# An eighteenth seven-product group, partial outputs kept in PSUM, and a port lock in the scheduler of a convolution-and-joint kernel

## The chip, the cores and the metric

The kernel runs on one core of one Trainium2 chip. Its time is the device time in microseconds (us). Before the change it is 260.56 us, the median of 3 runs (260.44 to 260.65).

## The reference

Two strided convolutions with gelu, then a "joint": every frame is added to every one of 8 label states, goes through tanh and one 512x512 product.

```python
B, T, D, K, U = 2, 4000, 512, 5, 8
h = gelu(conv5(x, w1))[:, ::2]            # 2000 frames
f = gelu(conv5(h, w2))[:, ::2]            # 1000 frames
fe = einsum("btd,de->bte", f, w_f)
ge = einsum("bud,de->bue", g, w_g)
j = tanh(fe[:, :, None, :] + ge[:, None, :, :])
return einsum("btud,dv->btuv", j, w_o)    # 16000 rows of 512
```

## The kernel before

All engines work from one list of operations. The program gives each operation a cost, a list scheduler plans the order on each engine, and semaphores follow from what is read and written. The joint's 16000 rows are 125 tiles of 128. A plain tile takes 4 matmuls of 512 columns. Four neighbouring tiles can also be done as a *group*: a seven-product scheme on 2x2 blocks, with 28 matmuls of 256 columns in place of 16 of 512, paid for by additions on other engines. `WQ` lists the groups done so. Groups below 14 have their operand sums on VectorE, the later ones on GpSimd (POOL). TensorE writes its products into PSUM, which the program uses as eight banks of 512 columns (tile name `acc`); the other engines copy or add them from there into SBUF, the working memory. Later products can add onto what a bank holds. The parts that matter here, cut:

```python
WQ = (5,6,10,11,12,13,16,17,18,20,21,22,23,24,26,27,28)      # 17 groups
LEAD, TRAIL = 4,4            # plain tiles ahead of and behind the late groups
...
def op(self, eng, fn, reads=(), writes=(), cost=0.1):         # one operation in the plan
...
        def quad_steps(q, eng, u=[0]):
            ...
            def sums():      # eight 128x256 (or four 128x512) additions, two SBUF inputs each
                ...
            def one():
                held.extend(banks.pop(0) for _ in range(3))
                x, y, z = held
                product(Ab(0, 0), Bb(0, 0), x, True)      # product: 4 matmuls of 256 columns
                product(Sb(1), Tb(1), y, True)
                act(k1, v2(x), ACT.Copy)
                tt("dve", u2, v2(y), k1, add)             # PSUM + SBUF -> SBUF
            def two():
                product(Sb(0), Tb(0), z, True)
                product(Ab(0, 1), Bb(1, 0), x, False)
                tt("dve", k15, v2(z), k1, add)
                act(half(0, 0), v2(x), ACT.Copy)          # half: a quarter of the output
            def three():
                product(Sb(2), Tb(2), y, False)
                product(Sb(3), Bb(1, 1), z, False)
                tt("dve", half(1, 1), v2(y), k15, add)
                tt("dve", half(0, 1), v2(z), u2, add)
            def four():
                product(Ab(1, 1), Tb(3), y, False)
                tt("dve", half(1, 0), v2(y), k1, add)
            return [sums, one, two, three, four]
...
        def joint_tile(jt):
            ...
                by_act = h == 1 if last else jt % 2 == 0 if end else jt % 3 == 2 if early else plain[0] % 3 == 2
                # the copy out of PSUM: by ScalarE if by_act, else by VectorE; then an output transfer
...
        def weights_o(wT):   # four sums of the joint's weights, on VectorE
```

The convolution units (`stages`) run on the same engines, with joint tiles as filling between their steps. `fe(0)` and `fe(1)` are the products with w_f.

Of the kernel before, what the change touches and what calls it, by code (L numbers as in the profile page):

```python
# [7 lines left out]
ACT = mybir.ActivationFunctionType  # L8
# [4 lines left out]
P = 128  # L13
# [3 lines left out]
class View:  # L17


    __slots__ = ("ap", "cells", "psum")  # L20
# [41 lines left out]


class Op:
    __slots__ = ("eng", "fn", "reads", "writes", "dma", "signal", "count", "sem", "val", "idx", "cost", "pin", "after", "nbytes", "rate")


class Plan:
# [11 lines left out]
    def op(self, eng, fn, reads=(), writes=(), cost=0.1):  # L80
        o = Op()
        o.eng, o.fn, o.dma, o.signal, o.idx = eng, fn, False, False, len(self.ops)
        o.reads, o.writes, o.cost, o.pin, o.after = tuple(reads), tuple(writes), cost, eng in self.pin, []
        self.ops.append(o)
        return o

    def dma(self, eng, fn, reads=(), writes=(), sem=None, nbytes=524288, rate=300e3):

        o = Op()
        o.eng, o.fn, o.dma, o.signal, o.idx = eng, fn, True, False, len(self.ops)  # L90
        o.reads, o.writes, o.after, o.nbytes = tuple(reads), tuple(writes), [], nbytes
        o.cost, o.pin = (1.35, False) if eng == "pool" else (0.05, True)
        o.rate = rate
        if sem is None:
            sem = [self.nc.alloc_semaphore(f"s_d{o.idx}"), 0]
        sem[1] += 16
        o.sem, o.val = sem[0], sem[1]
        self.ops.append(o)
        return o
# [91 lines left out]
    def simulate(self, pred, succ, late):  # L191


        ops, HOP = self.ops, self.HOP
        n = len(ops)
        left = [len(p) for p in pred]
        ready = [0.0] * n
        free = {e: 0.0 for e in ("pe", "act", "dve", "pool", "sp")}
        cand = {e: [] for e in free}
        for i in range(n):  # L200
            if not left[i]:
                cand[ops[i].eng].append(i)
        order = {e: [] for e in free}
        wire, soft, start = 0.0, 0.0, [0.0] * n
        for _ in range(n):
            best = None
            for e, c in cand.items():
                if c:
                    t = max(free[e], min([ready[i] for i in c]))
                    if best is None or t < best[0]:  # L210
                        best = (t, e)
            t, e = best
            now = [i for i in cand[e] if ready[i] <= t + 0.02]
            i = min(now) if e in ("pe", "sp") else min(now, key=lambda i: (late[i], i))
            cand[e].remove(i)
            order[e].append(i)
            o = ops[i]
            start[i] = t
            free[e] = t + o.cost
            end = free[e]  # L220
            if o.dma and e == "pool":
                soft = max(soft, end + 3.0)
                busy = wire > soft + 1.0
                soft += o.nbytes / (60e3 if busy else 230e3)
                wire += o.nbytes / 220e3 if busy else 0.0
                end = max(soft, end + 4.0)
            elif o.dma:
                wire = max(wire, t + 1.3) + o.nbytes / o.rate
                end = max(wire, t + 2.0)
            for s in succ[i]:  # L230
                ready[s] = max(ready[s], end + HOP if pred[s][i] else free[e])
                left[s] -= 1
                if not left[s]:
                    cand[ops[s].eng].append(s)
        return order, start, max(free.values())
# [75 lines left out]
def bass_standalone__seq2seq_rnn_t_joint__speech_kernel(  # L311
# [27 lines left out]
    XW = 528  # L339
    HOFF, HWID = 2, 338  # L340
    RING, LRING = 2048, 4096
    WQ = (5,6,10,11,12,13,16,17,18,20,21,22,23,24,26,27,28)
    LEAD, TRAIL = 4,4
    FROM, LATE = 64 * P, 30
    NSLOT = 12
    BU = B * U
# [4 lines left out]
    with ExitStack() as es:  # L351
# [163 lines left out]
        for pp in range(2):  # L515
            for rt in range(2):
                bk = 4 + 2 * pp + rt
                pv = View(psb[:, bk * 1024:(bk + 1) * 1024].rearrange("p (r k c) -> p r k c", r=2, k=NK), np.array([bk]), True)

                def fn(e, rt=rt, pp=pp, pv=pv):  # L520
                    for r in range(2):
                        for k in range(NK):
                            ins = e.transpose(pv.ap[:, r, k, :], xr[rt].h[:, 2 * r + pp, k, :], ident.h[:, :])
                    return ins
                pl.op("pe", fn, (xr[rt][:], ident[:]), (pv,), 0.8)
                o = xs[0][pp::2, :, 16 + rt * P:16 + (rt + 1) * P]
                if pp:
                    act(o, pv, ACT.Copy)
                else:
                    pl.op("dve", lambda e, o=o, pv=pv: e.tensor_copy(out=o.ap, in_=pv.ap), (pv,), (o,), vec_cost(o, (pv,)))  # L530


        def shift(src, off, dst, c0, n, which):
# [104 lines left out]

        banks = [0, 1, 2, 4]
        fbanks = [3, 5, 7, 6]  # L640
        class Tile_:
            def __init__(self, b, src, dst, c0, i0, n, keep=False):
                self.b, self.i0, self.n, self.keep = b, i0, n, keep
# [12 lines left out]
            def gelu(self, m, src):  # L656
                j = HOFF + self.i0 // 3
                o = hT[self.b][:, m, j:j + self.n // 3].map(
                    lambda a: a.rearrange("p (r s) q -> p s r q", s=2))
                src = src.map(lambda a: a.rearrange("p s (q r) -> p s r q", r=3))  # L660
                act(o, src, ACT.Gelu_apprx_tanh)

            def gelu1(self, m, s, src):
                j = HOFF + self.i0 // 3
# [53 lines left out]
        class Triple:  # L718
# [64 lines left out]
            def stages(self, m, split=None):  # L783
                n, u = self.n, post_n[0]
                post_n[0] += 1
                e, f_at = banks.pop(0), []
                E = ps.cols(e * NT, n)
                F = lambda: ps.cols(f_at[0] * NT, n)
                k1, k2, y = ((sd4[m] if split else sd[u % 2])[i, 0:n] for i in range(3))
# [16 lines left out]

                def two():
                    self.product("t2", m, e, False)
                    f_at.append(banks.pop(0))
                    stt("dve", F(), E, 2.0 * f_, k2)  # L810
                    tt("dve", k1, k1, k2, add)
                    stt("dve", y, E, f_, k1)
                    self.out(1, m, y)
# [157 lines left out]
        pl.pin = ()  # L971


        def bank():
            banks.append(banks.pop(0))
            return banks[-1] * NT

        def ge():
            c0 = bank()
            bank()  # L980
            for m in range(NK):
                mm(ps.cols(c0 + m * BU, BU), [(wg_sb[k, m * P:(m + 1) * P], gT[k]) for k in range(NK)], True, True)
            act(geT[:], ps.cols(c0, NK * BU), ACT.Copy)

        def fe(b):
            for i, m in ((1, 0), (0, 0), (1, 1), (0, 1), (2, 0), (2, 1), (1, 2), (0, 2), (2, 2), (1, 3), (0, 3), (2, 3)):
                v = ps.cols(bank(), START[i + 1] - START[i])
                sl = slice(START[i], START[i + 1])
                mm(v, [(wf_sb[k, m * P:(m + 1) * P], fT[b][k, sl]) for k in range(NK)], True, True)
                o = feT[b][m, i::3]  # L990
                if i == 1:
                    act(o, v, ACT.Copy, cost=0.45)
                else:
                    pl.op("dve", lambda e, o=o, v=v: e.tensor_copy(out=o.ap, in_=v.ap), (v,), (o,), 0.475)  # L994
# [72 lines left out]
        def joint_tile(jt):  # L1067
# [10 lines left out]
            for h in range(2 if last else 1):  # L1078
                w = NT // 2 if last else NT
                cl = slice(h * w, (h + 1) * w)  # L1080
                v = ps.cols(bank(), w)
                mm(v, [(j(k), wo_sb[k, cl]) for k in range(NK)], True, True)
                o = oste[s, cl] if s < 4 else ostq[s - 4, cl] if s < 16 else ostm[s - 16][cl]
                end = jt > ntile - 6
                by_act = h == 1 if last else jt % 2 == 0 if end else jt % 3 == 2 if early else plain[0] % 3 == 2
                if by_act:
                    act(o, v, ACT.Copy)
                else:
                    pl.op("dve", lambda e, o=o, v=v: e.tensor_copy(out=o.ap, in_=v.ap), (v,), (o,), vec_cost(o, (v,)))  # L1089
                send(c0, s, cl, "act" if end and by_act else "sp")  # L1090

        def weights_o(wT):
# [3 lines left out]
            tt("dve", T_[1], B_[1][1], T_[0], sub)  # L1096
            tt("dve", T_[2], B_[1][1], B_[0][1], sub)
            tt("dve", T_[3], B_[1][0], T_[1], sub)

        def quad_steps(q, eng, u=[0]):  # L1100

# [72 lines left out]
            def four():  # L1174
# [4 lines left out]
                banks.append(y)  # L1179
                send2(c0 + 2 * P, s1, s0 + 2)  # L1180

            return [sums, one, two, three, four]

        fes = [1]
        one_tile = lambda jt: (lambda: joint_tile(jt), 1)
        for q in range(14):
            if q in WQ:
                st = quad_steps(q, "dve")
                work.insert(len(work) - (1 if q < 8 else 3), (st[0], 0))
                if q == 13:  # L1190
                    work.append((lambda: weights_o(wT), 0))
                work.extend((f, 1) for f in st[1:])
            else:
                work.extend(one_tile(jt) for jt in range(4 * q, 4 * q + 4))
        left = [jt for jt in range(56, ntile) if jt // 4 not in WQ]
        lateq = [quad_steps(q, "pool") for q in WQ if q >= 14]
        n = len(lateq)
        stream = []
        for i in range(n + 1):
# [114 lines left out]
```

## Time and profile before

In the profile lines PE is TensorE's matmuls, PEld its weight loads (the stationary operands), DVE VectorE, ACT ScalarE, POOL GpSimd. A timeline line gives start and length in us, engine, source line, operation, tiles (written <- read), shape and count, and in brackets how long the engine stood idle before it and what released it; `...` marks lines left out. Tiles: `sA`, `sAm` are operand sums of groups, `wT`, `wTm` sums of the joint's weights, `kq`, `kqm` partial outputs kept in SBUF, `oste`, `ostq`, `ostm` outputs on their way out, `jT`, `jL` the joint's tanh values, `hT` and `fT` the convolutions' outputs, `sd`, `row` and `r` values between the convolutions' steps.

Stages are cut at starts of matmuls in the trace: *head* is from the span's start to the first fe(0) matmul, *middle* from there to the first fe(1) matmul (conv2 and the groups up to 13), *fe(1)* its own matmuls, *tail* from the last fe(1) matmul to the end of the last matmul, *end* from there to the end of the span.

| stage, us | before | before, run again |
|---|---|---|
| head | 79.11 | 78.85 |
| middle | 112.31 | 112.32 |
| fe(1) | 6.68 | 6.67 |
| tail | 57.71 | 57.85 |
| end | 2.83 | 2.83 |
| span | 258.64 | 258.52 |

### The profile page before, as it was taken

How to read it: one execution, taken by the hardware profiler on the slowest of the kernel's cores; microseconds unless marked ns; L12 is line 12 of the kernel's file. 1: busy time of each engine (PE TensorE's matmuls, PEld its weight loads, DVE VectorE, ACT ScalarE, POOL GpSimd, SP SyncE). 2: the span in 40 equal slices, each digit the busy share in tenths (PEclk: the TensorE clock that was granted, in tenths of full speed). 3: DMA queues.
4: the chain of work that ended last, by engine and by line, in shares of the span. 5: the costliest groups of instructions: out<-in, count | busy, mean ns of one | idle time of the engine just before them, and what ended most of it. 6: DMA issues, size and time to landing. Idle time of an engine off the chain costs nothing.

```text
span 258.6 us, 4891 instructions
## 1 busy us (share of the span) xinstructions
PE 252.5 (98%) x1772; PEld 171.4 (66%) x1786; DVE 227.1 (88%) x446; ACT 189.7 (73%) x317; POOL 56.0 (22%) x64
## 2 busy tenths in 40 slices
PE   8998999999999999999999999999999999999995
PEld 4897764446666556565677754777776677777772
DVE  1999999999999999999647899999957698898974
ACT  2778979975366999667765659848549999999631
POOL 1000004300000000000000000000001999999940
DMA  6999998979995022102111031404120264545457
GB/s 239 329 161 190 255 311 181 166 138 187 235 188 103 3 81 81 63 20 71 54 41 66 19 122 42 145 0 144 41 81 4 80 205 143 185 138 179 152 166 242
DMA packets 56277, 33.95 MB, mean 131 GB/s; under 512 B 31150, under 2 KB 55998, under 8 KB 56254
## 3 DMA queue, kind: packets, MB, share of 16 engines
q1 hardware_dynamic: 53710, 31.22, 45.2%
q0 software_dynamic: 2112, 2.10, 4.7%
q8 instruction: 14, 0.23, 0.4%
q10 hardware_dynamic: 432, 0.33, 0.4%
q14 instruction: 9, 0.07, 0.1%
HBM read 7.86 MB, written 16.38 MB: 94 GB/s over the span
## 4 chain that ended last, share of the span: by engine, by line
PE 88%; DMA 5%; SPq 3%; DVE 1%; issue 1%; ACT 0%; DVEq 0%
PE acc L430 88%; SPq L461 3%; DMA w_sb<-in_w_dram 2%; DMA xs<-in_x_dram 1%; DMA xr<-in_x_dram 1%; DMA out_dram<-ostq 1%; DVE kq L417 0%; DVE ty L598 0%; DVE xt L417 0%; DVE ostq L417 0%; DVE w_t L598 0%; ACT fT L422 0%; ACT cs L422 0%; ACT oste L422 0%; SPq L448 0%
## 5 line engine op out<-in xcount | busy, mean ns | idle before, releaser
L430 PE MATMUL acc<-wo_sb,jT 128*128 128x512 bf16 (+1 forms) x199 | 45.0, 353 | 0.5
L1147 POOL TENSOR_TENSOR sA<-jL 128x512 f16<-128x512 bf16 x22 | 25.1, 1158 | 87.5 <-ACT jL L422 85.4
L422 ACT ACTIVATE jT<-feT,geT 128x1000 bf16<-128x1000 f32 (+9 forms) x56 | 40.6, 779 | 3.2 <-PE acc L430 2.1
L422 ACT ACTIVATE jL<-feT,geT 128x1000 bf16<-128x1000 f32 (+3 forms) x36 | 35.8, 1054 | 0.6 <-DVE feT L994 0.6
L417 DVE TENSOR_TENSOR ostq<-acc,kq 128x512 bf16<-128x512 f32 x45 | 29.6, 682 | 3.2 <-PE acc L430 3.0
L430 PEld LDWEIGHTS acc<-wo_sb,jT 128*128 128x128 bf16 x208 | 20.2, 98 | 15.6 <-ACT jT L422 0.2
L430 PE MATMUL acc<-wo_sb,jL 128*128 128x256 bf16 (+1 forms) x155 | 28.9, 313 | 0.3
L430 PE MATMUL acc<-xt,w_sb 128*128 128x252 bf16 (+1 forms) x144 | 23.5, 305 | 0.0
L417 DVE TENSOR_TENSOR kq<-acc,kq 128x512 f32<-128x512 f32 x30 | 19.6, 683 | 3.9 <-PE acc L430 2.6
L422 ACT ACTIVATE hT<-acc 128x334 bf16<-128x334 f32 (+3 forms) x33 | 15.1, 465 | 10.1 <-PE acc L430 10.0
L1089 DVE CAST oste<-acc 128x512 bf16<-128x512 f32 (+1 forms) x25 | 16.9, 684 | 4.6 <-PE acc L430 4.5
L430 PE MATMUL acc<-row,w_sb 128*128 128x334 bf16 (+1 forms) x112 | 20.5, 305 | 0.0
L430 PEld LDWEIGHTS acc<-wo_sb,jL 128*128 128x128 bf16 x160 | 15.5, 98 | 7.1
L430 PE MATMUL acc<-wT,sA 128*128 128x256 f16 x144 | 20.1, 273 | 0.0
L422 ACT ACTIVATE sd<-acc 128x334 f32<-128x334 f32 (+1 forms) x32 | 13.9, 446 | 7.2 <-PE acc L430 6.9
L430 PEld LDWEIGHTS acc<-xt,w_sb 128*128 128x128 bf16 x144 | 14.0, 98 | 7.0 <-DVE xt L417 0.3
L430 PE MATMUL acc<-zx,w_sb 128*128 128x334 bf16 (+1 forms) x96 | 17.6, 305 | 0.0
L422 ACT ACTIVATE ostq<-acc 128x512 bf16<-128x512 f32 x20 | 12.5, 623 | 6.2 <-PE acc L430 3.8
L430 PEld LDWEIGHTS acc<-wT,sA 128*128 128x128 f16 x144 | 14.1, 98 | 3.8
L430 PE MATMUL acc<-xs,w_t 128*128 128x252 bf16 (+1 forms) x76 | 14.0, 314 | 0.7 <-ACT cs L422 0.7
L430 PE MATMUL acc<-row,w_t 128*128 128x334 bf16 (+1 forms) x80 | 14.6, 305 | 0.0
L414 POOL MEMSET zx<- 128x8 bf16 (+1 forms) x3 | 0.5, 150 | 64.8 <-PE acc L430 36.6
(130 smaller groups left out, 537.2 us busy)
## 6 DMA issues: line engine op xcount, KB each, us to landing
out_dram<-ostq SPq DMA_DIRECT2D x24, 256.0 KB, 2.3
w_sb<-in_w_dram SPq DMA_DIRECT2D x10, 512.0 KB, 5.7
out_dram<-oste SPq DMA_DIRECT2D x32, 128.0 KB, 1.9
out_dram<-ostq SPq DMA_DIRECT2D x19, 128.0 KB, 2.0
xr<-in_x_dram SPq DMA_DIRECT2D x2, 512.0 KB, 4.1
half<-w_sb POOLq DMA_DIRECT2D x2, 512.0 KB, 6.5
half<-w_t POOLq DMA_DIRECT2D x2, 512.0 KB, 5.2
out_dram<-oste SPq DMA_DIRECT2D x3, 256.0 KB, 2.1
```

Source lines behind the costliest of these rows:

```text
L414: pl.op("pool", lambda e: e.memset(v.ap, 0.0), (), (v,))
L417: pl.op(eng, lambda e: e.tensor_tensor(out=o.ap, in0=a.ap, in1=b.ap, op=op), (a, b), (o,), vec_cost(o, (a, b)))
L422: pl.op("act", lambda e: e.activation(o.ap, i.ap, func, scale=scale, bias=0.0 if bias is None else bias.ap), rd, (o,), cost or o.ap.free_s ...
L430: ins = e.matmul(o.ap, lhsT=l.ap, rhs=r.ap, start=start and n == 0, stop=stop and n == len(pairs) - 1, skip_group_check=not check)
L461: pl.dma("sp", lambda e: e.dma_start_transpose(out=dst.ap, in_=src), (), (dst,), nbytes=(hi - lo) * D * 2, rate=180e3)
L1089: pl.op("dve", lambda e, o=o, v=v: e.tensor_copy(out=o.ap, in_=v.ap), (v,), (o,), vec_cost(o, (v,)))
L1147: pl.op(eng, lambda e, v=v, a=a, b=b, op=op: e.tensor_tensor(out=v.ap, in0=a.ap, in1=b.ap, op=op), (a, b), (v,), cost)
```

## The change

Intent: save TensorE columns with an eighteenth group (14 and 15 join, 16 leaves); relieve VectorE in groups 5 and 6, which run between convolution units, by keeping partial outputs in PSUM (ScalarE copies a bank into another and later products accumulate on it) in place of additions, called the *b form* below (`one_b` to `four_b`); and tell the scheduler that GpSimd and two-input VectorE instructions exclude each other. Cut to its core:

```diff
+        o.lock = eng == "pool" and cost > 0.5 or eng == "dve" and sum(not v.psum for v in o.reads) > 1
...
+            if port > t + 0.02:
+                now = [i for i in now if not ops[i].lock] or now
...
+            if o.lock:
+                t = max(t, port)
+                port = t + o.cost
...
-    WQ = (5,6,10,11,12,13,16,17,18,20,21,22,23,24,26,27,28)
-    LEAD, TRAIL = 4,4
+    WQ = (5,6,10,11,12,13,14,15,17,18,20,21,22,23,24,26,27,28)
+    WB, BYDVE = (5,6), ()
+    LEAD, TRAIL = 2,4
...
-                    ... (pv,), (o,), vec_cost(o, (pv,)))          # a transpose's copy
+                    ... (pv,), (o,), 0.6)
-                act(o, src, ACT.Gelu_apprx_tanh)
+                act(o, src, ACT.Gelu_apprx_tanh, cost=0.47 if src.psum else 0.88)
...
+            def one_b():        # only for q in WB
+                ...             # x, c: new banks; a: one that a matmul has written in full
+                product(Ab(0, 0), Bb(0, 0), x, True)
+                act(v2(a), v2(x), ACT.Copy)               # PSUM -> PSUM
+                product(Sb(2), Tb(2), c, True)
+            def two_b():
+                product(Ab(0, 1), Bb(1, 0), x, False)
+                product(Sb(1), Tb(1), a, False)           # adds onto the copy
+                act(k1, v2(a), ACT.Copy)
+                copy(half(0, 0), v2(x), "act")
+            def three_b():
+                product(Sb(0), Tb(0), a, False)
+                act(u2, v2(a), ACT.Copy)
+                tt("dve", half(1, 1), v2(c), u2, add)
+            def four_b():
+                product(Sb(3), Bb(1, 1), a, False)
+                copy(half(0, 1), v2(a), "dve")
+                product(Ab(1, 1), Tb(3), c, False)
+                tt("dve", half(1, 0), v2(c), k1, add)
...
-                work.insert(len(work) - (1 if q < 8 else 3), (st[0], 0))
+                work.insert(len(work) - (0 if q == 6 else 1 if q < 8 else 3), (st[0], 0))
```

The rest (`full`, `take()`, `bank(n)`) keeps account of which bank has been written over its whole width.

More of the change, by code (lines that the diff above doesn't have):

```diff
@@ L64 @@
 class Op:
-    __slots__ = ("eng", "fn", "reads", "writes", "dma", "signal", "count", "sem", "val", "idx", "cost", "pin", "after", "nbytes", "rate")
+    __slots__ = ("eng", "fn", "reads", "writes", "dma", "signal", "count", "sem", "val", "idx", "cost", "pin", "after", "nbytes", "rate", "lock")
 class Plan:
@@ L92, in dma @@
         o.cost, o.pin = (1.35, False) if eng == "pool" else (0.05, True)
-        o.rate = rate
+        o.rate, o.lock = rate, False
         if sem is None:
@@ L203, in simulate @@
         order = {e: [] for e in free}
-        wire, soft, start = 0.0, 0.0, [0.0] * n
+        wire, soft, port, start = 0.0, 0.0, 0.0, [0.0] * n
         for _ in range(n):
@@ L341, in bass_standalone__seq2seq_rnn_t_joint__speech_kernel @@
     RING, LRING = 2048, 4096
-    WQ = (5,6,10,11,12,13,16,17,18,20,21,22,23,24,26,27,28)
-    LEAD, TRAIL = 4,4
+    WQ = (5,6,10,11,12,13,14,15,17,18,20,21,22,23,24,26,27,28)
+    WB, BYDVE = (5,6), ()
+    COPY = ("act", "dve")
+    LEAD, TRAIL = 2,4
     FROM, LATE = 64 * P, 30
@@ L529, in bass_standalone__seq2seq_rnn_t_joint__speech_kernel @@
                 else:
-                    pl.op("dve", lambda e, o=o, pv=pv: e.tensor_copy(out=o.ap, in_=pv.ap), (pv,), (o,), vec_cost(o, (pv,)))
+                    pl.op("dve", lambda e, o=o, pv=pv: e.tensor_copy(out=o.ap, in_=pv.ap), (pv,), (o,), 0.6)
         def shift(src, off, dst, c0, n, which):
@@ L640, in bass_standalone__seq2seq_rnn_t_joint__speech_kernel, with take @@
         fbanks = [3, 5, 7, 6]
+        full = set()
+        def take():
+            b = next((b for b in banks if b not in full), banks[0])
+            banks.remove(b)
+            full.discard(b)
+            return b
         class Tile_:
@@ L785, in stages @@
                 post_n[0] += 1
-                e, f_at = banks.pop(0), []
+                e, f_at = take(), []
                 E = ps.cols(e * NT, n)
@@ L808, in two @@
                     self.product("t2", m, e, False)
-                    f_at.append(banks.pop(0))
+                    f_at.append(take())
                     stt("dve", F(), E, 2.0 * f_, k2)
@@ L971, in bass_standalone__seq2seq_rnn_t_joint__speech_kernel, with bank @@
         pl.pin = ()
-        def bank():
+        def bank(n=NT):
             banks.append(banks.pop(0))
+            (full.add if n == NT else full.discard)(banks[-1])
             return banks[-1] * NT
         def ge():
-            c0 = bank()
-            bank()
+            c0 = bank(0)
+            bank(0)
             for m in range(NK):
@@ L986, in fe @@
             for i, m in ((1, 0), (0, 0), (1, 1), (0, 1), (2, 0), (2, 1), (1, 2), (0, 2), (2, 2), (1, 3), (0, 3), (2, 3)):
-                v = ps.cols(bank(), START[i + 1] - START[i])
+                v = ps.cols(bank(0), START[i + 1] - START[i])
                 sl = slice(START[i], START[i + 1])
@@ L1080, in joint_tile @@
                 cl = slice(h * w, (h + 1) * w)
-                v = ps.cols(bank(), w)
+                v = ps.cols(bank(w), w)
                 mm(v, [(j(k), wo_sb[k, cl]) for k in range(NK)], True, True)
@@ L1098, in weights_o, with copy @@
             tt("dve", T_[3], B_[1][0], T_[1], sub)
+        def copy(o, v, eng):
+            if eng == "act":
+                act(o, v, ACT.Copy)
+            else:
+                pl.op("dve", lambda e: e.tensor_copy(out=o.ap, in_=v.ap), (v,), (o,), vec_cost(o, (v,)))
         def quad_steps(q, eng, u=[0]):
@@ L1180, in four @@
                 send2(c0 + 2 * P, s1, s0 + 2)
+            def one_b():
+                x = banks.pop(0)
+                a = next((b for b in banks if b in full), None)
+                if a is None:
+                    a = banks[0]
+                    mm(ps.cols(a * NT, NT), [(zero[0:P], zero[:])], True, True)
+                banks.remove(a)
+                c = banks.pop(0)
+                full.update((x, a, c))
+                held.extend((x, a, c))
+                product(Ab(0, 0), Bb(0, 0), x, True)
+                act(v2(a), v2(x), ACT.Copy)
+                product(Sb(2), Tb(2), c, True)
+            def two_b():
+                x, a, c = held
+                product(Ab(0, 1), Bb(1, 0), x, False)
+                product(Sb(1), Tb(1), a, False)
+                act(k1, v2(a), ACT.Copy)
+                copy(half(0, 0), v2(x), COPY[0])
+                banks.append(x)
+            def three_b():
+                x, a, c = held
+                product(Sb(0), Tb(0), a, False)
+                act(u2, v2(a), ACT.Copy)
+                tt("dve", half(1, 1), v2(c), u2, add)
+            def four_b():
+                x, a, c = held
+                product(Sb(3), Bb(1, 1), a, False)
+                copy(half(0, 1), v2(a), COPY[1])
+                product(Ab(1, 1), Tb(3), c, False)
+                done.update(range(4 * q, 4 * q + 4))
+                tt("dve", half(1, 0), v2(c), k1, add)
+                banks.extend((a, c))
+                send2(c0, s1, s0)
+                send2(c0 + 2 * P, s1, s0 + 2)
+            if q in WB:
+                return [sums, one_b, two_b, three_b, four_b]
             return [sums, one, two, three, four]
@@ L1195, in bass_standalone__seq2seq_rnn_t_joint__speech_kernel @@
         left = [jt for jt in range(56, ntile) if jt // 4 not in WQ]
-        lateq = [quad_steps(q, "pool") for q in WQ if q >= 14]
+        lateq = [quad_steps(q, "dve" if q in BYDVE else "pool") for q in WQ if q >= 14]
         n = len(lateq)
```

## The prediction

> **What bounds the kernel now.** I read the page first (busy shares, slices, chain), then the waits of TensorE alone, then the timeline of TensorE, then busy time by stage.
>
> ```profile
> PE 252.5 (98%) x1772; PEld 171.4 (66%) x1786; DVE 227.1 (88%) x446; ACT 189.7 (73%) x317; POOL 56.0 (22%) x64
> ...
> PE   8998999999999999999999999999999999999995
> PEld 4897764446666556565677754777776677777772
> DVE  1999999999999999999647899999957698898974
> ...
> PE 88%; DMA 5%; SPq 3%; DVE 1%; issue 1%; ACT 0%; DVEq 0%
> ```
>
> TensorE is busy in every slice, and 88% of the chain that ended last is its matmuls. VectorE is full too in the first half, but it owns only 1% of the chain. A busy PE is not proof that it never waits, so the waits of PE come next; these are all of them:
>
> ```profile
> PE acc L430 <- DVE zero L437: 1.2, 1, 1.2
> PE acc L430 <- ACT cs L422: 0.7, 1, 0.7
> PE acc L430 <- DMA w_sb<-in_w_dram: 0.2, 1, 0.2
> PE acc L430 <- ACT fT L422: 0.2, 1, 0.2
> ```
>
> By the timeline these waits lie at 0, 22.8, 10.3 and 78.8 us. Nothing after 79 us is charged to another engine. The timeline of PE near the end shows that the matmuls also run at their full rate:
>
> ```profile
> 245.66 1.03 PE L430 MATMUL acc<-wo_sb,jL 128*128 128x512 bf16 x4
> 246.53 1.47 PE L430 MATMUL acc<-wT,sA 128*128 128x256 f16 x12
> 247.83 0.60 PE L430 MATMUL acc<-wo_sb,jL 128*128 128x256 bf16 x4
> ```
>
> The first column is the start. Four matmuls of 512 columns take 246.53 - 245.66 = 0.87 us, 217 ns each; twelve of 256 columns take 1.30 us, 108 ns each. (The lengths printed per row, 0.38 us for one of 512, include pipeline latency; only starts give the rate.) As a test I laid the program's matmuls from the end of the second fe product (start of the next at 198.24 us) to the last one side by side, 215.8 ns for 512 columns and 109.2 ns for 256: the last one should leave the array at 255.64 us. The trace has the last end at 252.18 + 3.63 = 255.81 us, which is that plus the 0.16 us by which the printed end of a matmul trails the next start. So in its last 57 us TensorE waits for nothing at all, and only fewer columns, or the 2.8 us of evacuation and output transfer after 255.8, can shorten it. Small gaps of some 216 ns that the timeline seems to show are matmul records missing from the trace (1772 records for 1787 matmuls).
>
> **What the Trainium skill says.** "TensorE: Matmul & The Clock Gate", section "Wait — 56ns, not 53.3ns?": warm matmuls start N / 2.4 GHz plus about 2.5 ns apart. That gives 215.8 and 109.2 ns; the trace agrees (217 and 108). "SBUF — State Buffer", section "Who interferes with whom": VectorE and GpSimd share a port pair under an exclusive lock. A VectorE instruction with two SBUF inputs is in that class. The trace of before cannot test it: the POOL sums run 197.4 to 248.8 us, at 1147 to 1181 ns each, while VectorE there reads one operand from PSUM. "PSUM — Partial Sum Buffer", section "The four PSUM rules": writes by ScalarE leave the accumulate bits alone, and a matmul without the clear flag adds onto such data where an earlier matmul wrote the element. The changed groups rest on this and the kernel before doesn't use it, so no run yet shows it.
>
> **The change, part by part.** I compared the two programs' instructions engine by engine.
>
> *Columns.* 16 matmuls of 512 columns go, 28 of 256 come; nothing else changes on TensorE. This is the swap of seven-product groups: group 16 leaves, 14 and 15 join, so 18 in place of 17. A group of four plain tiles costs 4 x 4 x 215.8 ns = 3.45 us, a seven-product group 28 x 109.2 ns = 3.06 us. Saved: 0.39 us (with the timeline's 217 and 108 ns, 0.45). The zeroing matmul in the new code, for the case that no bank is marked full, is not emitted even once.
>
> *Groups 5 and 6 (about 131 to 149 us).* Their 28 matmuls each stay. VectorE loses 4 additions into kqm (686 ns) and 2 into oste (683 ns) and gets 2 copies (about 690 ns, from the plain tiles' copies): 4.1 - 1.4 = 2.7 us less. ScalarE gets 2 copies from PSUM to PSUM and 2 more into kqm: 4 x 588 ns = 2.4 us more. Neither is on the path: between 125 and 150 us PE is busy 24.95 of 25.00 us, VectorE 17.2, ScalarE 15.3. Worth nothing by itself; it makes bank and VectorE room. It adds chains, though: the product into the copied bank must wait for the copy, and the next one for the copy out. In the timeline of before the first product of group 5 starts at 131.64, and the place that now holds the product onto the copy at 135.23: some 3 us for a 0.59 us copy. The next distance is shorter: product done at about 135.83, its follower at 136.81 with one ScalarE copy between, some 0.2 to 0.3 us to spare.
>
> *Sums of groups 14 and 15.* They go to POOL, 16 instructions of 128x256; four instructions of 128x512 (group 16) leave. An estimate from the measured 1157 ns for 512 columns is 0.58 us for 256, so 9.3 us come and 4.6 go. In before POOL idles until 197.4 us, then runs without a break to 248.8 us; the new sums mostly fall into that idle time.
>
> *Port lock in the scheduler.* With the re-estimated costs beside it (three of them), it changes orders only. Up to about 110 us all five engines keep their order, but for ScalarE, which does one copy ahead of one gelu at 28.7 us and moves a weight scaling by 2 us at 31.6 us; PE runs full there in before. So the start, where the real PE waits lie, keeps its cost. TensorE's own order first differs at about 132 us. The last three plain tiles and their output transfers stay as they are, so the 2.8 us at the end stay.
>
> *Sum.* -0.39 us on TensorE, 0 elsewhere, against 260.56 us: 260.17. I add 0.05 us for a small wait or two that the tighter chains may open, and say 260.2 us, 0.15% faster.
>
> **The rivals.**
>
> 1. *The first sums from jL come late.* In before the first jL operand enters TensorE 5.6 us after 198.24 us, now 2.2 us after. Its last quarter needs the last feT copy (ends about 199.1 us), then two short tanh pieces placed ahead and one of 808 columns, so about 200.4 us; TensorE asks for it at about 200.4 + 3 x 0.216 = 201.1. Half a microsecond is left. POOL can begin group 17 at about 204.2 us (after the sums of 15); its fifth instruction, at 1.115 us from start to start, ends at about 209.8, and TensorE asks for it at 210.4. Again 0.6 us. If one fails I expect 0.3 to 1 us: 260.5 to 261.2.
> 2. *POOL's new sums and VectorE lock each other out.* Between 140 and 191 us VectorE is busy 48.5 of 51.4 us and feeds the conv2 units, so each blocked addition of two SBUF operands may wait up to 0.58 us. The new sums have some 20 us before TensorE needs them, and the scheduler now knows of the lock; but a model's plan is not the chip's. If eight collided, VectorE would fall behind by up to 4.6 us, of which perhaps 1 us would reach TensorE: 261.2.
> 3. *VectorE was the true limit and its relief pays more.* Against it: TensorE's waits after 27 us total under 1 us, most of it at 79 and 88 us, before anything changes. At most 0.2 us more could come back: 259.95.
>
> **Range and chances.** The downside (1 and 2) is longer than the upside (3), while repeats of before spread 0.2 us. So 259.85 to 260.75 for 8 in 10. A move of 2% is 5.2 us: for faster there is no idle time to recover; for slower several waits would have to open at once. Faster 0.01, same 0.98, slower 0.01.
>
> **What would show it.** Right: PE's busy time about 0.4 us shorter, PE's waits the same four rows, the second fe product ending at the same time within 0.1 us and the last matmul about 0.4 us earlier; POOL's first sum before 197 us; VectorE about 2.7 us less busy in the stage of groups 5 and 6. Wrong: a new PE wait on ACT acc or kqm near 137 us (the copy chain), on ACT jL or POOL sA between 200 and 211 us (rival 1), on DVE sd or acc between 150 and 191 us with POOL rows or two-input VectorE rows lengthened (rival 2), or an earlier end of the second fe product (rival 3).

## The result, and the profile after

The changed kernel is correct and takes 259.8 us (median of 6 runs, 259.60 to 260.43) against 260.49 us (6 runs, 260.22 to 260.65) for the kernel before in the same rounds. The ratio is 0.9979, 95% interval 0.9966 to 0.9993: 0.55 us or 0.2% faster, well within 2%. Ratios here are the mean time of one kernel's fast runs over the mean of the other's fast runs of the same rounds, so they are not quite the ratio of the medians quoted.

The page of the changed kernel, with busy time by engine, the slices of three engines, and the chain that ended last:

```profile
PE 251.9 (98%) x1783; PEld 173.0 (67%) x1798; DVE 226.7 (88%) x444; ACT 192.0 (75%) x322; POOL 62.3 (24%) x76
...
PE   8999999999999999999999999999999999999995
PEld 4897764446666556566677755777777777777863
DVE  1999999999999999999636899999977798898984
...
PE 85%; DMA 5%; ACT 5%; DVE 3%; issue 2%; ACTq 0%; DVEq 0%
```

Little here looks different: TensorE is full in every slice before and after, and its busy time fell by 0.6 us (16 records are missing in this trace, 15 in the other, so that figure is rough). Shares of a span cannot explain a change of 0.2%. The waits of TensorE in the changed kernel:

```profile
PE acc L438 <- DVE zero L445: 1.2, 1, 1.2
PE acc L438 <- ACT tc L430: 0.3, 1, 0.3
PE acc L438 <- ACT fT L430: 0.2, 1, 0.2
```

No row came after the head: neither the copy chain of groups 5 and 6 nor the first sums from jL are in it. All three lie in the first 80 us, with the head's scatter. The stage table says where the time went:

| stage, us | before | changed | changed, run again | step (middle, tail, end) |
|---|---|---|---|---|
| head | 79.11 | 78.49 | 78.90 | scatter |
| middle | 112.31 | 112.04 | 112.02 | -0.28 |
| fe(1) | 6.68 | 6.67 | 6.67 | 0 |
| tail | 57.71 | 57.31 | 57.31 | -0.40 |
| end | 2.83 | 2.98 | 2.99 | +0.15 |
| span | 258.64 | 257.49 | 257.89 | |

The repeatable steps sum to -0.40 - 0.28 + 0.15 = -0.53 us, which agrees with the measured ratio (-0.55 us; its interval runs from -0.18 to -0.89). The 1.15 us between the two profiled spans is half chance: 0.62 us of it is the head.

**The tail** is the predicted saving: 16 x 215.8 ns - 28 x 109.2 ns = 0.40 us, and TensorE still runs there at its full rate. From the timeline of PE in the changed kernel (starts in the first column):

```profile
246.54 0.60 PE L438 MATMUL acc<-wT,sA 128*128 128x256 f16 x4
246.98 1.03 PE L438 MATMUL acc<-wo_sb,jL 128*128 128x512 bf16 x4
247.84 0.60 PE L438 MATMUL acc<-wo_sb,sA 128*128 128x256 bf16 x4
```

Four of 256 columns in 0.44 us, four of 512 in 0.86 us, as before.

**The middle** held a wait that the prediction says does not exist ("Nothing after 79 us is charged to another engine"). The list of waits has a second part, for the weight loads of TensorE (PEld), and this is a row of it in the kernel before, followed by the timelines of PEld and of VectorE around it:

```profile
PEld acc L430 <- ACT sd L422: 0.8, 2, 0.6
```

```profile
159.92 0.67 PEld L430 LDWEIGHTS acc<-wo_sb,jT 128*128 128x128 bf16 x4
161.19 0.41 PEld L430 LDWEIGHTS acc<-hT,w_t 128*128 128x128 bf16 x4 [0.59 <-ACT sd L422]
```

```profile
158.22 0.68 DVE L1089 CAST oste<-acc 128x512 bf16<-128x512 f32 x1
158.82 0.98 DVE L417 TENSOR_TENSOR hT<-hT 128x668 bf16<-128x668 bf16 x3
159.72 0.49 DVE L417 TENSOR_TENSOR row<-r 128x334 bf16<-128x334 f32 x1
160.14 0.98 DVE L417 TENSOR_TENSOR hT<-hT 128x668 bf16<-128x668 bf16 x3
```

The weights for acc<-hT,w_t came 0.59 us late. The releaser named, ScalarE's sd, had ended at 160.71; what ends just before 161.19 is VectorE's last hT<-hT sum (160.14 + 0.98 = 161.12). VectorE was late there by one or two instructions. The timeline of PE shows why its own rows do not have the wait:

```profile
160.06 1.03 PE L430 MATMUL acc<-wo_sb,jT 128*128 128x512 bf16 x4
161.22 0.73 PE L430 MATMUL acc<-hT,w_t 128*128 128x334 bf16 x4
```

The printed end of the first line, 161.09, trails the start that the next matmul could have had by 0.16 us, so only 0.13 us of idle time is left to see, less than any row in the list of waits. From start to start, 1.16 us passed where four matmuls of 512 columns take 0.87. It cost TensorE 0.29 us. In the changed kernel the same sums start earlier and the loads follow without a wait (timelines of VectorE and PEld):

```profile
157.03 1.88 DVE L425 TENSOR_TENSOR hT<-hT 128x668 bf16<-128x668 bf16 x6
```

```profile
159.25 0.60 PEld L438 LDWEIGHTS acc<-hT,w_t 128*128 128x128 bf16 x4
159.89 0.67 PEld L438 LDWEIGHTS acc<-wo_sb,jT 128*128 128x128 bf16 x4
```

**GpSimd** starts its new sums at 175.82 us (predicted: before 197). **The end** grew by 0.15 us; the last experiments are about that.

### The profile page after: what moved, and what is told of

Read it like the earlier page. It is cut to its first block, busy times and chain, and to the rows that moved or that the text cites. A ratio compares the mean times of both kernels' runs of the same rounds, so it can differ in the third digit from the quotient of the medians.

```text
span 257.5 us, 4938 instructions
## 1 busy us (share of the span) xinstructions
PE 251.9 (98%) x1783; PEld 173.0 (67%) x1798; DVE 226.7 (88%) x444; ACT 192.0 (75%) x322; POOL 62.3 (24%) x76
## 4 chain that ended last, share of the span: by engine, by line
PE 85%; DMA 5%; ACT 5%; DVE 3%; issue 2%; ACTq 0%; DVEq 0%
PE acc L438 85%; DMA w_sb<-in_w_dram 4%; ACT jL L430 2%; DVE w_t L606 2%; DMA xr<-in_x_dram 1%; ACT jT L430 0%; ACT w_sb L430 0%; ACT kq L430 0%; ACT oste L430 0%; DVE ty L606 0%; DVE feT L1011 0%; DVE ws L425 0%; ACT feT L430 0%; DVE xt L425 0%; ACT ostq L430 0%
## 5 line engine op out<-in xcount | busy, mean ns | idle before, releaser
L438 PE MATMUL acc<-wo_sb,jT 128*128 128x512 bf16 (+1 forms) x185 | 39.8, 342 | 0.4
L425 DVE TENSOR_TENSOR ostq<-acc,kq 128x512 bf16<-128x512 f32 x48 | 31.7, 685 | 4.6 <-PE acc L438 4.5
L430 ACT ACTIVATE jL<-feT,geT 128x1000 bf16<-128x1000 f32 (+3 forms) x36 | 34.9, 1057 | 0.6 <-DVE feT L1011 0.6
L438 PE MATMUL acc<-wo_sb,jL 128*128 128x256 bf16 (+1 forms) x160 | 30.9, 320 | 0.4
L438 PEld LDWEIGHTS acc<-wo_sb,jT 128*128 128x128 bf16 x192 | 18.7, 98 | 13.3 <-ACT jT L430 0.2
L1170 POOL TENSOR_TENSOR sA<-jL 128x512 f16<-128x512 bf16 x20 | 22.8, 1165 | 0.2 <-ACT jL L430 0.2
L425 DVE TENSOR_TENSOR kq<-acc,kq 128x512 f32<-128x512 f32 x32 | 21.4, 683 | 1.5 <-ACT kq L430 0.8
L1170 POOL TENSOR_TENSOR sA<-jT 128x256 f16<-128x256 bf16 x4 | 2.6, 670 | 79.4 <-PE acc L438 64.6
L438 PE MATMUL acc<-wT,sA 128*128 128x256 f16 x156 | 21.6, 273 | 0.0
L438 PEld LDWEIGHTS acc<-wT,sA 128*128 128x128 f16 x156 | 15.3, 98 | 3.1
```

The lines of the kernel that those rows point to most:

```text
L425: pl.op(eng, lambda e: e.tensor_tensor(out=o.ap, in0=a.ap, in1=b.ap, op=op), (a, b), (o,), vec_cost(o, (a, b)))
L430: pl.op("act", lambda e: e.activation(o.ap, i.ap, func, scale=scale, bias=0.0 if bias is None else bias.ap), rd, (o,), cost or o.ap.free_s ...
L438: ins = e.matmul(o.ap, lhsT=l.ap, rhs=r.ap, start=start and n == 0, stop=stop and n == len(pairs) - 1, skip_group_check=not check)
L1170: pl.op(eng, lambda e, v=v, a=a, b=b, op=op: e.tensor_tensor(out=v.ap, in0=a.ap, in1=b.ap, op=op), (a, b), (v,), cost)
```

## The experiments

Theory after the result: the columns give 0.40, VectorE's relief in groups 5 and 6 gives 0.29, the lock is worth nothing, 18 groups cost 0.15 at the end. Rivals: the difference is chance; the lock is worth more than that; the b form itself is not what closes the wait. Twelve kernels ran, four on one chip each, 5 rounds each, all correct. Medians of the kernel before in the three calls: 260.39, 260.12 and 260.15 us. A ratio's interval is about 0.12 to 0.22% wide to either side, up to 0.57 us, so the stage tables decide where the rounds cannot.

| run | ratio (95% interval) | middle | tail | end |
|---|---|---|---|---|
| aa_before | 1.0001 (0.9980 to 1.0022) | 112.32 | 57.85 | 2.83 |
| after_again | 0.9980 (0.9961 to 0.9999) | 112.02 | 57.31 | 2.99 |
| q17 | 0.9975 (0.9958 to 0.9991) | 112.02 | 57.71 | 2.82 |
| wq_only | 1.0036 (1.0017 to 1.0055) | 113.25 | 57.31 | 2.96 |
| before_t28 | 0.9999 (0.9986 to 1.0012) | 112.02 | 57.71 | 2.84 |
| nolock | 1.0034 (1.0022 to 1.0046) | 113.03 | 57.31 | 2.98 |
| q19_8_1 | 0.9982 (0.9969 to 0.9994) | 111.74 | 57.31 | 3.44 |
| nob_t28 | 0.9984 (0.9970 to 0.9998) | 112.03 | 57.31 | 2.98 |
| nolock_late | 0.9988 (0.9976 to 1.0000) | 112.04 | 57.36 | 2.98 |
| nocost | 0.9986 (0.9974 to 0.9998) | 112.03 | 57.31 | 2.97 |
| q19_t5 | 1.0008 (0.9996 to 1.0020) | 111.74 | 57.31 | 4.18 |
| after_t5 | 1.0020 (1.0007 to 1.0032) | 112.03 | 57.31 | 3.68 |

**aa_before and after_again: the two kernels once more, unedited.** How much do the parts repeat?

> The kernel before, unchanged, against itself. Any theory: ratio 1.000, the interval shows the noise. Head theory A (the 0.6 us by which the first 27 us of the changed kernel were shorter is chance of when the input transfers land): this profile may show the first matmul after the first four conv1 units of tile 0 at anything between 26.3 and 27.0 us, and the times of single runs spread over 0.6 us or more. Head theory B (the change shortens the head): always close to 26.98 us, spread 0.4 us at most. The wait of TensorE before the conv2 units at about 160.7 us (0.3 us) should be there again.

> The changed kernel, unchanged. Steady part (fe of batch 1 to the last matmul) 57.16 us again against 57.57; the stretch between the two fe products 112.04 against 112.31 us. If those two are the whole effect (0.40 us of columns, 0.28 us of a closed wait) the ratio is 0.9974, 0.68 us; with the head as a third true part of 0.6 us it would be 0.995; with columns alone, as predicted, 0.9985.

Medians 260.38 and 259.98 us. The middle, the end and the changed kernel's tail repeat to 0.02 us, the head to 0.41. The 0.2% is real and the head's part of it is not.

**q17: the changed code with the old 17 groups.**

```diff
-    WQ = (5,6,10,11,12,13,14,15,17,18,...)
-    LEAD, TRAIL = 2,4
+    WQ = (5,6,10,11,12,13,16,17,18,...)
+    LEAD, TRAIL = 4,4
```

> Changed kernel without the eighteenth group: seventeen groups and four leading tiles as before, but groups 5 and 6 with copies, the port lock and the new cost figures. Theory: the wait of 0.3 us at about 160.7 us is gone, last stretch as long as before (57.57 us): 0.28 us faster, ratio 0.9989. Rival (my prediction: groups 5 and 6 are worth nothing): ratio 1.000, wait still there.

Median 259.70 us. The tail is back at 57.71, the end at 2.82, and the middle stays at 112.02. So the 0.40 us in the tail and the 0.15 us at the end both belong to the eighteenth group, and the 0.29 us in the middle belongs to the rest of the change. The round ratio is lower than expected; it lies within the interval of the changed kernel's. By the rounds alone q17 is not slower than the changed kernel (259.70 against 259.98 us in after_again), so the net 0.25 us of the eighteenth group is read from the stages and not shown by the times.

**wq_only: the kernel before with nothing but the 18 groups.**

```diff
-    WQ = (5,6,10,11,12,13,16,17,18,...)
-    LEAD, TRAIL = 4,4
+    WQ = (5,6,10,11,12,13,14,15,17,18,...)
+    LEAD, TRAIL = 2,4
```

> The kernel before with the eighteen groups and two leading tiles, nothing else. Theory: 0.40 us from the columns alone, last stretch 57.16 us, the wait at 160.7 us still there: ratio 0.9985. Rival (the eighteenth group needs the lock in the scheduler and the copies to be fed): new TensorE waits between 198 and 211 us, ratio 1.000 or above.

Median 261.39 us: slower than before by 0.36%. The theory failed here. The tail is 57.31 as it should be, but the middle is 113.25, 0.93 us longer than in the kernel before. Besides the old wait at 161 us (still in its list, 0.6 us) the list of PE has a new one, of 0.74 us, at 186.35 us and not between 198 and 211 as the rival had it:

```profile
PE acc L430 <- DVE ostq L417: 0.7, 1, 0.7
```

The columns alone lose time; something else in the change holds a loss back.

**before_t28: the kernel before, one copy out of PSUM (tile 28) moved from VectorE to ScalarE.**

```diff
-                ... else jt % 3 == 2 if early else ...
+                ... else (jt % 3 == 2 or jt == 28) if early else ...
```

> The kernel before with one edit: the copy out of plain tile 28 is done by ScalarE in place of VectorE (0.7 us of VectorE work less just after group 6). Theory (the wait of TensorE at 160.7 us is VectorE running late with the operands of the first conv2 unit): the wait shrinks or goes, the stretch between the two fe products 112.04 us in place of 112.31, ratio 0.9989. Rival (the form of groups 5 and 6, with its free banks, is what closes it): wait unchanged, ratio 1.000.

Median 260.00 us. The rounds can't resolve it. The trace can: the middle is 112.02. With one 0.68 us copy less in front of them, the sums that were late start 0.60 us earlier (heads aligned) and the weight load has no wait (timelines of VectorE and PEld):

```profile
157.55 1.88 DVE L417 TENSOR_TENSOR hT<-hT 128x668 bf16<-128x668 bf16 x6
```

```profile
160.04 0.60 PEld L430 LDWEIGHTS acc<-hT,w_t 128*128 128x128 bf16 x4
```

So VectorE was indeed the releaser, and 0.68 us of relief was enough, not the 2.7 that the prediction worked out for groups 5 and 6. The edit also let the scheduler change orders: the row sum that stood between the six hT sums runs behind them here, as in the changed kernel, so the last one ends 1.02 us earlier, and ScalarE's sd copy runs earlier, too. How much of that each part was needed for is not separated; sd had ended 0.48 us before the late load.

**nob_t28: the changed kernel without the b form, with that copy moved.**

```diff
-    WB, BYDVE = (5,6), ()
+    WB, BYDVE = (), ()
-                ... else jt % 3 == 2 if early else ...
+                ... else (jt % 3 == 2 or jt == 28) if early else ...
```

> The changed kernel with groups 5 and 6 in their old form, and tile 28 copied by ScalarE in place of VectorE. Theory (VectorE's load before 160 us is all that the new form is worth): same as the changed kernel, 0.9974 of before, no wait at 160.7 us. Rival: that wait is back, ratio 0.9985.

Median 259.59 us, and every stage after the head equals the changed kernel's within 0.02 us. The whole PSUM-to-PSUM machinery can be replaced by one moved copy. The b form alone taken out, without the moved copy, did not run.

**nolock: the changed kernel without the lock and with the old cost figures.**

```diff
-        o.lock = eng == "pool" and cost > 0.5 or eng == "dve" and sum(not v.psum for v in o.reads) > 1
+        o.lock = False
-        ... 0.6)
+        ... vec_cost(o, (pv,)))
-        act(o, src, ACT.Gelu_apprx_tanh, cost=0.47 if src.psum else 0.88)
+        act(o, src, ACT.Gelu_apprx_tanh, cost=None)
```

> The changed kernel without the port lock and without the new cost figures in the scheduler. TensorE's, POOL's and the queue's order are the same as in the changed kernel, only a few VectorE and ScalarE instructions trade places. Theory: same time as the changed kernel, 0.9974 of before. Rival (the lock is what lets POOL's sums of groups 14 and 15 pass): waits of TensorE between 175 and 210 us, ratio 0.998 to 1.000.

Median 261.04 us, middle 113.03: the theory, and the prediction's worth of 0 for "changes orders only", are wrong by 1.0 us. TensorE, GpSimd and the output queue have the same order as in the changed kernel. Only VectorE (around 178 to 188 us) and a little of ScalarE differ. There is a wait that neither kernel had (waits of PE, then the timeline of PE):

```profile
PE acc L438 <- DVE ostq L425: 0.8, 1, 0.8
```

```profile
185.03 0.73 PE L438 MATMUL acc<-row,w_sb 128*128 128x334 bf16 x4
186.59 0.61 PE L438 MATMUL acc<-wTm,jT 128*128 128x256 f16 x4 [0.83 <-DVE ostq L425]
```

TensorE waits for a bank that VectorE's addition into ostq frees. The timelines of VectorE and GpSimd before it:

```profile
178.96 0.95 DVE L1170 TENSOR_TENSOR sA<-jT 128x256 f16<-128x256 bf16 x2
179.84 0.95 DVE L1170 TENSOR_TENSOR sA<-jT,sA 128x256 f16<-128x256 bf16 x2
...
183.49 0.95 DVE L1170 TENSOR_TENSOR sA<-jT,jT 128x256 f16<-128x256 bf16 x2
...
185.86 1.28 DVE L425 TENSOR_TENSOR ostq<-acc,kq 128x512 bf16<-128x512 f32 x2
```

```profile
179.06 0.71 POOL L1170 TENSOR_TENSOR sA<-jT,jT 128x256 f16<-128x256 bf16 x1 [1.59 <-DVE ostq L425]
179.84 0.80 POOL L1170 TENSOR_TENSOR sA<-sA,jT 128x256 f16<-128x256 f16 x1
180.72 1.02 POOL L1170 TENSOR_TENSOR sA<-jT,sA 128x256 f16<-128x256 bf16 x1
```

Group 14's sums on GpSimd run beside VectorE's own two-input sums, and both get longer: a pair on VectorE takes 0.95 us, and GpSimd's instructions reach 1.02 us where the others take 0.67. In the single records the two engines take turns: of each pair on VectorE one instruction takes 274 to 279 ns and the other 750 to 753 ns, ending 0.15 us after the GpSimd instruction that was running. Three such pairs cost VectorE 3 x 0.47 = 1.42 us.

One doubt is left: without the lock VectorE has another order, which might be late at any speed.

**nolock_late: the same kernel; only GpSimd's sums of group 14 wait until VectorE's two-input work is over.**

```diff
-   pl.op(eng, ... (a, b), (v,), cost)
+   r = pl.op(eng, ... (a, b), (v,), cost)
+   if q == 14:
+       r.after.extend(pl.hold)      # last sum of group 13, last addition into wT
```

> The kernel without the port lock in its plan (and with the old costs), with one thing changed: GpSimd's sums of group 14 must wait for VectorE's last sum of group 13 and its last addition into wT, so that they run from about 190 us on, beside copies out of PSUM, and not from 176 to 184 us beside VectorE's two-input sums. TensorE, VectorE, ScalarE and the output queue keep every instruction in the order of the kernel without the lock; only GpSimd waits. Theory (GpSimd and VectorE hold each other up at the shared ports, and that alone cost the 1 us): VectorE's two-input sums of jT back to about 280 ns in place of 515, the wait of 0.8 us on the ostq addition at 185 to 186.6 us gone, the middle stage 113.03 us -> 112.02 to 112.1, ratio to before 1.0034 -> 0.997 to 0.9985. Rival (the order on VectorE without the lock puts the ostq addition behind the sums, and would be late at any speed): the wait stays, middle stage above 112.7, ratio 1.002 or more. A mix: between. Tail 57.31 in all.

Median 259.87 us (the ratio, 0.9988, is 0.0003 above the expected range). The middle is 112.04; the whole 1.0 us is back. The tail was expected at 57.31 and is 57.36: a weight load at 233.78 us waits 0.16 us for ScalarE's copy into ostq, which costs TensorE 0.05 us. TensorE, VectorE, ScalarE and the output queue have exactly nolock's order. The timelines of VectorE, GpSimd and PE:

```profile
178.80 0.48 DVE L1172 TENSOR_TENSOR sA<-jT 128x256 f16<-128x256 bf16 x2
179.20 0.49 DVE L1172 TENSOR_TENSOR sA<-jT,sA 128x256 f16<-128x256 bf16 x2
...
184.27 1.29 DVE L425 TENSOR_TENSOR ostq<-acc,kq 128x512 bf16<-128x512 f32 x2
```

```profile
188.21 1.29 POOL L1172 TENSOR_TENSOR sA<-jT,jT 128x256 f16<-128x256 bf16 x2 [76.78 <-DVE wT L425]
```

```profile
185.51 0.60 PE L438 MATMUL acc<-wTm,jT 128*128 128x256 f16 x4
```

VectorE's pairs take 0.48 us, the ostq addition starts 1.59 us earlier (1.50 when the traces are aligned at 176 us), and TensorE does not wait. The collision, and not the order, was the cause. GpSimd could start its sums 12 us later at no cost to the middle: only the moment was wrong.

**nocost: the changed kernel, lock kept, old cost figures.**

```diff
-        ... 0.6)
+        ... vec_cost(o, (pv,)))
-        act(o, src, ACT.Gelu_apprx_tanh, cost=0.47 if src.psum else 0.88)
+        act(o, src, ACT.Gelu_apprx_tanh, cost=None)
```

> The changed kernel with its lock, but with the scheduler's old figures for the transposes' copies and the gelu. Against the changed kernel only ScalarE's order differs, in two spots before 35 us; TensorE, VectorE and GpSimd are the same. Theory (the cost figures are worth nothing by themselves): middle 112.02, tail 57.31, ratio 0.997 to 0.9985 as the changed kernel, so that the whole step to the kernel without lock and costs is the lock. Rival (the costs matter): head over 79.3 us or middle over 112.3, ratio over 0.9995.

Median 259.79 us, stages as the changed kernel's. The re-estimated costs are worth nothing that can be measured, and nolock's 1.0 us is the lock's alone.

**q19_8_1: a nineteenth group (8) in the b form, with its sums placed one step earlier, and tile 28's copy on ScalarE.**

```diff
-    WQ = (5,6,10,11,...)
-    WB, BYDVE = (5,6), ()
+    WQ = (5,6,8,10,11,...)
+    WB, BYDVE = (5,6,8), ()
-                work.insert(len(work) - (0 if q == 6 else 1 if q < 8 else 3), (st[0], 0))
+                work.insert(len(work) - (1 if q == 8 else 0 if q == 6 else 1 if q < 8 else 3), (st[0], 0))
```

> The changed kernel with a nineteenth group (8, in the form with copies) and tile 28 copied by ScalarE. By columns another 0.40 us: ratio 0.9959 of before if TensorE stays fed. If VectorE, nearly full at 150 to 165 us, falls behind, a wait there eats 0.1 to 0.6 us: 0.996 to 0.998.

Median 259.49 us, ratio 0.9982, above both expectations. The middle is 0.28 us shorter than the changed kernel's in place of 0.40; most of the rest is a new wait of a weight load at 159.27 us (0.28 us, ScalarE's kq named as releaser), which costs TensorE 0.10 us. The end is 3.44 us in place of 2.98 and takes the gain back.

**after_t5 and q19_t5: five plain tiles kept for the end in place of four**, in the changed kernel and in q19_8_1.

```diff
-    LEAD, TRAIL = 2,4
+    LEAD, TRAIL = 2,5
```

> The changed kernel with five plain tiles kept for the end in place of four. Theory (as for 19 groups): the end falls from 2.98 to about 2.83 us as in the kernel before; middle 112.02, tail 57.31; ratio 0.9973 to 0.998. Rival: end stays within 0.05 us of 2.98, ratio as the changed kernel's.

> The kernel with 19 groups, with five plain tiles kept for the end in place of four. With four its TensorE stages were shorter by 0.28 us than the changed kernel's, but the stretch from the last matmul to the end grew from 2.98 to 3.44 us and took all of it back. Theory (the last stretch is set by how many output bytes are still queued, and by their order): end 2.85 to 3.05 us, middle 111.74, tail 57.31 to 57.35, ratio 0.9965 to 0.9975, the best so far. Rival (the order of the last sends does not matter, or the last transfer is slow for another reason): end stays at 3.3 to 3.5, ratio 0.998.

Medians 260.68 and 260.25 us. Both expectations failed, in the same direction: the end did not shrink, it grew to 3.68 and 4.18 us. This is what the DMA view says of the stretch from the last matmul to the end, in the kernel before, the changed one, q19_8_1, after_t5 and q19_t5 (one line each, in five fences):

```profile
DMA packets 510, 0.33 MB, mean 116 GB/s; under 512 B 64, under 2 KB 510, under 8 KB 510
```

```profile
DMA packets 734, 0.53 MB, mean 177 GB/s; under 512 B 90, under 2 KB 734, under 8 KB 734
```

```profile
DMA packets 775, 0.57 MB, mean 167 GB/s; under 512 B 96, under 2 KB 774, under 8 KB 774
```

```profile
DMA packets 1019, 0.80 MB, mean 217 GB/s; under 512 B 112, under 2 KB 1019, under 8 KB 1019
```

```profile
DMA packets 1035, 0.82 MB, mean 197 GB/s; under 512 B 112, under 2 KB 1034, under 8 KB 1034
```

Their ends are 2.83, 2.98, 3.44, 3.68 and 4.18 us: the more output is still to be moved when the last matmul is done, the later the end. In after_t5, where the queue does not run empty before it is done, the first 24 slices of that view lie between 301 and 445 GB/s, most of them near 350; the Trainium skill, "DMA: Bandwidth & Descriptors", section "Specifications", gives about 358 GB/s as the limit of the HBM per core, which agrees in size. That it is this limit is not shown, but at such a rate bytes take time.

A guess at where they come from: a group hands over four tiles at once where plain tiles hand over one at a time, so an order with more of them near the end would leave more in the queue. That the bytes are the cause was not isolated (no run cut the last transfers alone), and the sizes do not fit them alone: from the kernel before to the changed one 0.20 MB come, which is 0.57 us at 350 GB/s, and the end grew by 0.15 (in the kernel before the queue runs empty meanwhile); from there to q19_8_1 0.04 MB come, some 0.1 us, and the end grew by 0.46.

The two kernels with 19 groups end with a trickle of some 20 GB/s for about half a microsecond. Their views alone list one more packet, of kind "instruction": in q19_8_1 it has 8192 bytes, starts at 255.45 us and takes 0.78 us; from its end at 256.23 us on 512-byte packets of output follow one by one, 24 ns apart, until 256.62 us. That this fetch held up one of the 16 DMA engines is likely and not shown. Three plain tiles at the end, or the last group's transfers in smaller pieces, remain to be tried. No run beat the changed kernel by more than its scatter.

## Why the prediction was right or wrong

The class was right, and so was the time (260.2 us, range 259.85 to 260.75): the measured ratio, applied to the 260.56 us from which the prediction starts, gives 260.01. (The median of the later rounds, 259.80, lies just under the range; the kernel before was at 260.49 there.) The gain is 0.55 us for a predicted 0.39 less a wait of 0.05. The mechanism was right in part, and that the total fell so near is luck in part. By its own steps:

- *Columns, -0.39 us*: right. The tail is 57.31 us in the kernels with 18 groups (57.36 in nolock_late), 0.40 us shorter than before, and unchanged in q17.
- *"TensorE waits for nothing at all" in the last 57 us*: right for the trace that it reads; the repeat loses 0.13 us there. *"Nothing after 79 us is charged to another engine"*: right as a reading of the PE rows, wrong as a statement about TensorE. The wait of 0.59 us at 161 us stood in the PEld rows, which were not read. (The times given for the four waits are 0.2 to 0.3 us early: the longest but one begins at 23.03 us and not at 22.8.)
- *Groups 5 and 6, worth 0*: mis-sized, -0.29 us, because of that missed wait. The relief itself came as predicted: four additions into kqm and two into oste are gone and two copies came. But VectorE's busy time between 125 and 150 us fell only from 17.16 to 16.02 us; two copies of plain tiles, 0.7 us each, now run before 161 us where they ran later. before_t28 shows that a quarter of the predicted relief was enough. The feared copy chain did not show, and the changed kernel's correct result agrees with what the prediction quotes of the skill on adding onto a copied bank.
- *Sums of groups 14 and 15*: the estimate of 0.58 us each was low, they take 0.67 when nothing disturbs them, and GpSimd's busy time grew by 6.3 us in place of 4.7. And only half of them ran in what was idle time: group 15's eight start at 198.23 us. In the kernel before GpSimd does not run "without a break" from 197.4 us, it stands idle for 2.06 us at 198.6. None of this cost anything.
- *Port lock, "it changes orders only", worth 0*: this is the step that failed. Against the kernel before it gains nothing, since that kernel had no sums on GpSimd before 197 us. But the eighteenth group brings them, and without the lock it costs 1.0 us (nolock against nocost: middle 113.03 against 112.03). The change would then have been slower, as wq_only is. The sum was nearly right because the loss and its cure are in one change and cancel.
- *Rival 2 (the engines lock each other out)*: its mechanism is real. Its size was estimated as eight collisions, 4.6 us on VectorE and 1 us on TensorE; nolock shows three of 0.47 us, 1.42 us on VectorE and 1.0 us on TensorE, because TensorE was waiting for the bank that an ostq addition behind them frees. Its 261.2 us is close to nolock's 261.04. With the lock some collisions remain (one wT sum takes 883 ns in place of 403, one pair 0.97 us in place of 0.49) but at places where nobody waits.
- *Rival 1 (jL sums late)*: did not occur; the tail lost nothing.
- *Rival 3 (relief pays more, at most 0.2 us)*: came true with 0.29 us. Its cap was drawn from the PE rows, too.
- *"the 2.8 us at the end stay"*: wrong by +0.15 us. The program's last sends were the same, but not what was queued ahead of them.

So two misses of opposite sign (-0.29 and +0.15) are what separates 0.39 from 0.53.

## What to carry to other kernels

Read the waits of the weight loads along with those of the matmuls before calling TensorE free of waits: a late stationary operand shows only there. When work is moved to GpSimd, look for the VectorE instructions with two SBUF inputs that will run beside it, and ask which of them someone waits for; moving the GpSimd work in time costs nothing where it has slack. And in a kernel that writes much, count the bytes still queued when the last matmul ends, since a faster middle can be paid back there.

## What the Trainium skill lacked or had wrong

- "SBUF — State Buffer", section "Who interferes with whom": it states that a VectorE instruction with two SBUF inputs and a GpSimd instruction that reads SBUF block each other for a whole instruction. The runs agree; the page has no number for this pair. Here a 128x256 sum on VectorE took 750 to 753 ns in place of 274 to 279 behind a GpSimd sum of 707 to 899 ns, and the GpSimd ones grew from 670 to up to 1017 ns.
- "Perfetto Trace Analysis", section "Identifying the Most-Contended Engine": it recommends the busy share of the weight loads (with the share of peak arithmetic) over that of the matmuls as a measure of how near TensorE is to its limit. That share was 66% before and 67% after and told nothing here; what told was a wait of 0.59 us in the weight loads' own row, which the section doesn't mention as something to look for.
- No page that I read has a rule for the end of a kernel: 0.33, 0.53, 0.57, 0.80 and 0.82 MB still moving after the last matmul went with 2.83, 2.98, 3.44, 3.68 and 4.18 us to the end.
